# A gated Fourier mix and windowed attention on one core: when loads, subtractions and gates are listed

## The chip, the cores and the metric

The kernel runs on one core of a Trainium2 chip. The metric is device microseconds (us) of that core for one execution, as the median of several runs; lower is better. Engines are named as in the profile: PE is TensorE's matrix multiplication and PEld its load of weights, DVE is VectorE, ACT is Scalar (ScalarE), POOL is GpSimd, SP is SyncE, which issues nearly all DMAs.

## The reference

The input x has 2048 rows of 512 columns. Two results are mixed row by row with a gate g:

```python
# Fourier part: real part of a two-dimensional DFT, by matrices
a = x @ dft_hid_re.T ;  b = x @ dft_hid_im.T
y1 = dft_seq_re @ a - dft_seq_im @ b
# attention part: 32 heads of 16, causal, window of 256
q, k, v = split(x @ wqkv)
p = softmax(where(0 <= i - j < 256, q @ k.T / 4, -1e9))
y2 = (p @ v) @ wo
g = sigmoid((x * gate_w).sum(-1, keepdims=True))
out = g * y1 + (1 - g) * y2
```

All of it is float32.

## The kernel before, in words

**Split products.** A float32 matrix is split into a high part in the format fp32r (Scalar's cast, `hi_of`, line 84) and a low part, matrix minus high part (`lo_of`, line 87, on VectorE or GpSimd). A product is then three multiplications: high by high, high by low, low by high (`TERMS`, line 31).

**Two streams of work.** The attention runs over 128 steps n (8 groups of heads times 16 blocks of 128 rows). In each step `s_head` (line 312) multiplies q by k for the maxima of the rows, which VectorE reduces (line 328), and, nine steps later (`LAG`), `t_head` (line 372) multiplies again with the maxima in the matrix, Scalar takes exponentials (line 382), GpSimd masks (lines 388 and 392), and `pv` (line 396) multiplies by v. The dense part (`dense`, line 513) is a generator that yields after every matrix multiplication, and `fill` (line 733) takes a quota of its multiplications into each step of the attention. The dense part makes in turn: q, k and v (`qk_proj`, `v_proj`), b = -x times the imaginary matrix (`ab_proj` with i = 1, written to DRAM as `ab_scr1_0` to `ab_scr1_15`, 128x1024 each, high part beside low part), the other q and k, a (`ab_proj` with i = 0, of which twelve tiles stay in SBUF in `big`), then 16 row blocks of the first sequence matrix times a (`c_block`, the last two as a pair in `c_pair`), kept in DRAM as `r_scr0`, and 16 of the second times b. The sequence matrices come in pieces of 128x1024 (`raw`, `piece_load`), split by `piece_split` (line 453). Last come the rows of the output: attention times wo (`wo_run`, line 689), mixed with the gate, and stored.

**Order.** The program order is written out by the kernel itself. A clock `now` counts ticks: one for each dense multiplication, 0.7 for each quarter of a step. `defer(ticks, fn, ...)` (line 65) lists a function that many ticks later. Each engine works through its own instructions in that order. All `ld` (line 77) are on SyncE, so a DMA that must wait for a buffer or for one of the eight queues' earlier transfers holds those listed behind it.

**Places that matter here.**
- *b's tiles.* The last pair of blocks of the first matrix (`c_pair(0, 14, ..., True)`) frees the tiles of a one after the other. At chunk k, `load_next` is deferred by 5k ticks (line 506) and loads the tile of b whose number is `SC[k]`; `SC` is 4, 5, ..., 15, 0, 1, 2, 3 (line 466). TensorE's first use is in `c_pair(1, 0, ...)`, in that order.
- *Ring loads.* q and k of a group of heads are written to DRAM (`qk_scr`) by `qk_evict` (line 231) from a tile `hl`, of which there are three. `ring_load` (line 265) reads them, laid out by head, into `ring0` and `ring1`, in eight DMAs, for 512 rows of one group, ahead of their use. `m_rows` (line 332) writes the rows' maxima to `m_scr` in four DMAs and reads them back into the ring 20 ticks later.
- *Splits of pieces.* `split_raw` (line 94) lists two casts and two subtractions on halves of 512 columns at distances given by `at_` and `step`; with `pool` 1 GpSimd takes the first subtraction and VectorE the second, with 2 GpSimd takes both. The first pieces have `pool` 1: `piece_split(1, 1, 2)` and `piece_split(2, 9, 3)` (lines 582 and 583).
- *Gates.* `gate` (line 178) multiplies 512 columns of a row block of x by gate_w with a running sum, on VectorE, two in every second `sb` at ticks 3 and 7 (lines 567 to 569); `gate_exp` and `gate_end` make g from the sums.
- *wo.* `wo_load` (line 638) loads a quarter of wo and lists its split 20 and 23 ticks later.
- *Start.* Three warm-up multiplications on a tile of zeros (line 127), then `qk_first` (line 240): the first q and k, in 24 multiplications over four pieces of x of 128 columns (`XT[dk, 0]`, tiles `big`) and four pieces of the weights (`wq0`, tiles `hi` and `lo`), all split. Scalar makes the high parts, VectorE x's low parts, GpSimd the weights' low parts. GpSimd then fills a part of `ring1` with ones (line 157).
- *End.* `wo_run` for row block 15: twelve multiplications of 512 columns, one instruction of VectorE (line 706), one store.

Of the kernel before, what the change touches and what calls it, by code (L numbers as in the profile page):

```python
# [35 lines left out]
def fnet_window_mix(ctx: ExitStack, tc: tile.TileContext, xT, x, wqk, wv, wr, wi, cr, ci, wo, gw, out):  # L36
# [83 lines left out]
    def pt_tile(shape, dt=F32):  # L120
        return at.tile(shape, dt, name="pt", tag="pt", bufs=NPT)
# [17 lines left out]

    wraw = pt_tile([P, 1024])  # L140
    wq0 = [st.tile([P, 1024], F32R, name=h) for h in ("hi", "lo")]
    for dk in range(DK):
        c = slice(dk * 256, dk * 256 + 256)
        nc.scalar.dma_start(wraw[:, c], wqk[0][:, c])
    load_x_first(0)
    for dk in range(DK):
        c = slice(dk * 256, dk * 256 + 256)
        t = XT[dk, 0] = big.tile([P, 2, 512], F32R, name="big")
        raw = XRAW.pop((dk, 0))
        hi_of(wq0[0][:, c], wraw[:, c])  # L150
        hi_of(t[:, 0], raw)
        lo_of(wq0[1][:, c], wraw[:, c], wq0[0][:, c], True)
        lo_of(t[:, 1], raw, t[:, 0])

    ring = [const.tile([P, 2, S], F32R, name=f"ring{i}") for i in range(2)]
    for h in range(2):
        nc.gpsimd.memset(f(ring[1][64 * h + 32:64 * h + 64]), 1.0)

# [7 lines left out]

    gl = const.tile([P, 16], F32, name="gl")
    g1 = const.tile([P, 16], F32, name="g1")
# [8 lines left out]

    def gate(tb):
        t = GX[tb // 2][:, HALVES[tb % 2]]
        nc.vector.scalar_tensor_tensor(t, t, 1.0, gwb, op0=OP.mult, op1=OP.mult,  # L180
                                       accum_out=gl[:, tb:tb + 1])
        if tb == 15:
            defer(8, gate_exp)

    def gate_exp():
        e = const.tile([P, 16], F32, name="ge")
        nc.scalar.activation(e, gl, AF.Exp, scale=-1.0)
        defer(8, gate_end, e)
# [5 lines left out]

    rows = [False]

    def acc():
        return [ps_d.tile([P, 512], F32, name=f"d{h}", tag=f"d{h}", bufs=2) for h in range(1 + rows[0])]

# [40 lines left out]
    def qk_first(w):  # L240
        accs = [acc() for _ in range(2)]
        n = 0
        for t, dk in zip((0, 0, 1, 0, 2, 1, 0, 2, 1, 2, 1, 2), (0, 1, 0, 2, 0, 1, 3, 1, 2, 2, 3, 3)):
            a, b = ((0, 0), (1, 0), (0, 1))[t]
            for i in range(2):
                c = dk * 256 + i * 128
                mm(accs[i], w[a][:, c:c + 128], XT[dk, 0][:, b], n == 0, n == 11)
            n += 1
        return accs
# [15 lines left out]
    def ring_load(g, ss):  # L265
        sl = slice(ss * 512, (ss + 1) * 512)
        for h in range(2):
# [245 lines left out]
    def dense():  # L513
        wraw = [load_raw(wv[i]) for i in range(2)]
# [3 lines left out]
        wvs = [split_raw(r) for r in wraw]  # L518
        for i in range(2):
# [17 lines left out]
        for g in range(1, NG):  # L537
# [23 lines left out]
            if g == 1:  # L561
                for sb in range(16):
# [75 lines left out]
    def wo_load(g):  # L638
# [50 lines left out]
    def wo_run():  # L689
# [9 lines left out]
        r = wo_r.pop(tb)  # L699
        ps = ps_a.tile([P, 512], F32, name="t", tag="st")  # L700
        n = 0
        for g in range(NG):
            for a, b in TERMS:
                mm([ps], OHL[sb][g][:, a, c * P:(c + 1) * P], WO[g][b], n == 0, n == 11)
                n += 1
        nc.vector.scalar_tensor_tensor(r, ps, g0[:, tb:tb + 1], r, op0=OP.mult, op1=OP.add)
        defer(3, ld, out[tb], r)
        if c == 3:
# [121 lines left out]
```

## Time and profile before

| | |
|---|---|
| median of 3 runs | 816.08 us (815.92 to 816.9) |
| the profiled execution | 818.41 us, of which the span of recorded work is 816.7 us |
| PE busy | 799.0 us, 98% of the span |
| PEld / DVE / ACT / POOL busy | 691.9 / 484.7 / 436.6 / 421.9 us |
| moved by DMA | 164.06 MB, 201 GB/s over the span |
| mean granted clock of TensorE | 0.998 of full speed |

In the profile a row such as `549.73 9.40 SPq L78 DMA_DIRECT2D ring<-qk_scr x8` is the start and the duration in us, the engine or its queue (`SPq` is SyncE issuing), the line, the operation, output and inputs by the program's names, and how many instructions are joined in the row. Brackets such as `[3.11 <-DMA big<-ab_scr]` hold the time for which the engine had been idle, and what it was waiting for. In the view of waits the columns are: who waits for whom, us in total, how many times, the longest.

### The profile page before, as it was taken

The page shows a single profiled execution, that of the slowest core. Times are in us where ns is not written, and L with a number is a line of the kernel's source. Part 1 is how long each engine was busy: PE and PEld are TensorE (multiplying, and loading weights), DVE is VectorE, ACT ScalarE, POOL GpSimd, SP SyncE. Part 2 cuts the span into 40 slices and gives each one's busy share as a digit, 9 for nine tenths or more (in the row PEclk, how much of TensorE's full clock was granted, in tenths as well). Part 3 has the DMA queues.
Part 4 walks back from the last instruction along what each step waited for, and adds up shares of the span by engine and source line. Part 5 has one row for each costly group of instructions (what it writes and reads, how often), then busy time and mean ns, then how long its engine had stood idle before and what let it go on. Part 6 is the DMA issues. An engine that isn't in the chain of part 4 may idle for free.

```text
span 816.7 us, 22895 instructions
## 1 busy us (share of the span) xinstructions
PE 799.0 (98%) x8706; PEld 691.9 (85%) x8706; DVE 484.7 (59%) x1427; ACT 436.6 (53%) x892; POOL 421.9 (52%) x692
## 2 busy tenths in 40 slices
PE   9999999999999999999999999996999999999998
PEld 6789988889888988889888888984899988888886
DVE  4288878887776675546655655453655572245552
ACT  6334766667766665656666556553555555523110
POOL 6002666566666665666566666553666567600000
PEclk9999999999999999999999999999999999999999
DMA  7766687786885256657755554889665646478882
GB/s 277 252 173 205 199 280 245 258 266 215 250 255 179 61 165 176 187 163 194 222 148 143 163 152 129 266 268 297 180 175 141 177 127 195 161 239 259 269 239 84
DMA packets 92046, 164.06 MB, mean 201 GB/s; under 512 B 35296, under 2 KB 35936, under 8 KB 91808
## 3 DMA queue, kind: packets, MB, share of 16 engines
q1 hardware_dynamic: 90496, 160.50, 64.6%
q10 hardware_dynamic: 1440, 2.10, 0.7%
q8 instruction: 69, 1.13, 0.6%
q14 instruction: 41, 0.34, 0.2%
HBM read 109.84 MB, written 57.16 MB: 204 GB/s over the span
## 4 chain that ended last, share of the span: by engine, by line
PE 88%; DMA 6%; SPq 2%; DVE 1%; issue 1%; ACT 0%; POOL 0%; ACTq 0%; DVEq 0%; POOLq 0%
PE d L206 56%; PE d L202 9%; PE o L407 8%; PE t L202 5%; PE t L381 5%; PE s L325 4%; SPq L78 2%; DMA ring<-qk_scr 2%; DMA big<-ab_scr 2%; DMA qk_scr<-hl 1%; DMA raw<-x 1%; PE t L127 1%; DMA es<-wo 1%; DVE sm L328 1%; DMA ring<-m_scr 0%
## 5 line engine op out<-in xcount | busy, mean ns | idle before, releaser
L206 PE MATMUL d<-big,hi 64*128 64x512 f32 x2240 | 392.2, 395 | 6.7 <-DMA big<-ab_scr 6.6
L328 DVE CUSTOM_DVE_ANT_0 sm<-s,mask 128x384 f32<-128x384 f32 (+2 forms) x512 | 270.6, 529 | 143.8 <-PE s L325 83.9
L382 ACT ACTIVATE pt<-t 128x384 f32<-128x384 f32 (+2 forms) x512 | 237.7, 471 | 167.6 <-PE t L381 89.2
L206 PEld LDWEIGHTS d<-big,hi 64*128 64x128 f32 x2240 | 233.5, 186 | 32.4 <-DMA big<-ab_scr 9.6
L206 PE MATMUL d<-big,lo 64*128 64x512 f32 x1120 | 240.6, 393 | 0.0
L388 POOL TENSOR_SCALAR_AFFINE_SELECT pt<-pt 128x256 f32<-128x256 f32 x256 | 109.5, 428 | 180.8 <-ACT pt L382 164.2
L87 POOL TENSOR_TENSOR lo<-raw,hi 128x512 fp32r<-128x512 f32 x118 | 153.0, 1307 | 25.6 <-ACT hi L84 25.2
L381 PE MATMUL t<-ring,ring 50*128 50x384 f32 (+2 forms) x512 | 162.9, 329 | 3.2 <-ACT pt L382 1.4
L325 PE MATMUL s<-ring,ring 48*128 48x384 f32 (+2 forms) x512 | 163.1, 327 | 2.1 <-DVE nm L328 2.1
L206 PEld LDWEIGHTS d<-big,lo 64*128 64x128 f32 x1120 | 124.0, 186 | 11.5 <-issue 0.2
L206 PE MATMUL d<-hi,big 64*128 64x512 f32 x656 | 119.7, 392 | 0.0
L325 PEld LDWEIGHTS s<-ring,ring 48*128 48x128 f32 x512 | 92.3, 184 | 12.1 <-DVE nm L328 4.6
L381 PEld LDWEIGHTS t<-ring,ring 50*128 50x128 f32 x512 | 91.2, 184 | 11.7 <-ACT pt L382 2.2
L84 ACT CAST hi<-raw 128x512 fp32r<-128x512 f32 x146 | 87.4, 616 | 9.2 <-issue 7.9
L392 POOL TENSOR_SCALAR_AFFINE_SELECT pt<-pt 128x256 f32<-128x256 f32 x224 | 91.6, 409 | 0.0
L87 POOL TENSOR_TENSOR hl<-es,hl 128x512 fp32r<-128x512 f32 x34 | 44.8, 1319 | 72.7 <-ACT hl L84 68.9
L206 PEld LDWEIGHTS d<-hi,big 64*128 64x128 f32 x656 | 76.1, 186 | 5.8 <-issue 0.2
L206 PE MATMUL d<-lo,big 64*128 64x512 f32 x328 | 76.2, 394 | 0.0
L407 PEld LDWEIGHTS o<-pt,vpad 64*32 64x32 f32 x2816 | 60.1, 106 | 18.6 <-issue 4.6
L407 PE MATMUL o<-pt,vpad 64*32 64x320 f32 (+5 forms) x2816 | 74.0, 348 | 0.0
L414 DVE TENSOR_TENSOR os<-o,os 128x512 f32<-128x512 f32 x32 | 22.1, 691 | 70.3 <-ACT os L413 68.7
L211 ACT ACTIVATE es<-d 128x512 f32<-128x512 f32 x69 | 41.2, 597 | 25.0 <-PE d L206 22.7
(64 smaller groups left out, 705.4 us busy)
## 6 DMA issues: line engine op xcount, KB each, us to landing
qk_scr<-hl SPq DMA_DIRECT2D x32, 512.0 KB
ring<-qk_scr SPq DMA_DIRECT2D x128, 128.0 KB
raw<-cr SPq DMA_DIRECT2D x32, 512.0 KB
raw<-ci SPq DMA_DIRECT2D x32, 512.0 KB
ab_scr<-hl SPq DMA_DIRECT2D x20, 512.0 KB
big<-ab_scr SPq DMA_DIRECT2D x20, 512.0 KB
ring<-qk_scr SPq DMA_DIRECT2D x128, 64.0 KB
u_scr<-os SPq DMA_DIRECT2D x32, 256.0 KB
```

The lines of the kernel that those rows point to most:

```text
L84: nc.scalar.copy(hi, raw)
L87: (nc.gpsimd if pool else nc.vector).tensor_sub(lo, raw, f(hi))
L202: nc.tensor.matmul(pss[0], w, x, start=start, stop=stop)
L206: nc.tensor.matmul(pss[h], w[r], x[r], start=start, stop=stop)
L211: nc.scalar.activation(t, pss[0], AF.Copy, scale=scale)
L325: nc.tensor.matmul(ps[:, :w], ring[0][r, p, jb * P:(jb + 1) * P], ring[1][r, p, k0:k0 + w], start=True, stop=True)
L328: nc.vector.tensor_tensor_reduce(out=sm[:, :w], in0=ps[:, :w], in1=mask[:, WIN - w:], scale=1.0, scalar=3e38, op0=OP.add, op1=OP.min, accu ...
L381: nc.tensor.matmul(ps[:, :w], ring[1][r, p, q0:q0 + P], ring[0][r, p, q0:q0 + w], start=True, stop=True)
L382: nc.scalar.activation(pt[:, j, :w], ps[:, :w], AF.Exp, scale=-1.0)
L388: nc.gpsimd.affine_select(a, a, pattern=[[0, 2], [1, P]], compare_op=OP.is_ge, fill=0.0, base=0, channel_multiplier=-1)
L392: nc.gpsimd.affine_select(a, a, pattern=[[0, 2], [-1, P]], compare_op=OP.is_gt, fill=0.0, base=0, channel_multiplier=1)
L407: nc.tensor.matmul(ot[h][32 * j:32 * j + 32, a - sb * 512:e - sb * 512], v2[r, j], pt[r, j, a - kb * P:e - kb * P], start=kb == kbs[0], st ...
```

## The change

It has seven edits; none changes what is computed, apart from rounding in the first piece.

1. b's tile of chunk k is deferred by 4k ticks, not 5k.
2. `ring_load` lists its first four DMAs as before and, except for the first group, the other four 9.5 ticks later.
3. In `split_raw`, VectorE's subtractions of a deferred split are two quarters of 256 columns, two ticks apart. Pieces 1 and 2 are split at other distances: (1, 5) and (20, 5) for `at_` and `step`, where (1, 2) and (9, 3) stood.
4. A gate's row block is done in two halves of 256 columns, each with a sum of its own, at ticks 1, 4, 7 and 10 for two row blocks; one addition joins the sums at the end.
5. wo's split is listed 32 and 35 ticks after its load.
6. At the start, piece 0 of x and of the weights is multiplied unsplit (in float32, from the tiles `pt` that the loads fill), ahead of the rest; its split, still needed later, comes last. For pieces 1 to 3, VectorE casts x's high part and subtracts the weights' low parts, and GpSimd subtracts x's low parts. The filling of `ring1` with ones is taken apart: one half now stands ahead of these on GpSimd, one behind. The accumulators of a single product now take turns between two sets of PSUM buffers (`acc`).
7. The last row block of the output is done in two halves of 256 columns: twelve multiplications, one instruction of VectorE and one store each.

The diff, cut to its core:

```diff
-                if step:
+                if step and fn is lo_of and not args[3]:
+                    for q in range(2):
+                        k = slice(256 * q, 256 * q + 256)
+                        defer(at_ + step * (n + 2) + 2 * q, fn, *(t[:, k] for t in args[:3]))
+                elif step:
...
+    ones(0)
...
+    for dk in range(1, DK):
         c = slice(dk * 256, dk * 256 + 256)
...
+        hi_of(wq0[0][:, c], wqraw[:, c])
+        nc.vector.tensor_copy(t[:, 0], x_raw[dk])
+        lo_of(wq0[1][:, c], wqraw[:, c], wq0[0][:, c])
+        lo_of(t[:, 1], x_raw[dk], t[:, 0], True)
+        if dk == 1:
+            hi_of(XT[0, 0][:, 0], x_raw[0])
+            hi_of(wq0[0][:, :256], wqraw[:, :256])
+    lo_of(XT[0, 0][:, 1], x_raw[0], XT[0, 0][:, 0])
+    lo_of(wq0[1][:, :256], wqraw[:, :256], wq0[0][:, :256], True)
+    ones(1)
...
+    def gate(tb, q):
+        t = GX[tb // 2][:, tb % 2 * 512 + q * 256:tb % 2 * 512 + q * 256 + 256]
+        nc.vector.scalar_tensor_tensor(t, t, 1.0, gwb[:, q * 256:q * 256 + 256], op0=OP.mult, op1=OP.mult,
+                                       accum_out=gl[:, q, tb:tb + 1])
...
+    def gate_sum():
+        nc.vector.tensor_add(gl[:, 0], gl[:, 0], gl[:, 1])
...
+        for i in range(2):
+            mm(accs[i], wqraw[:, i * 128:i * 128 + 128], x_raw[0], True, False)
+        for a, b, dk in ((0, 0, 1), (1, 0, 1), (0, 1, 1), (0, 0, 2), (1, 0, 2), (0, 0, 3), (0, 1, 2), (1, 0, 3), (0, 1, 3)):
...
+        half(0)
+        if g:
+            defer(9.5, half, 1)
+        else:
+            half(1)
...
-                        defer(5 * k, load_next, SC[k])
+                        defer(4 * k, load_next, SC[k])
...
-                        defer(3, gate, sb - 1)
-                        defer(7, gate, sb)
+                        for q in range(4):
+                            defer(1 + 3 * q, gate, sb - 1 + q // 2, q % 2)
...
-        piece_split(1, 1, 2)
-        piece_split(2, 9, 3)
+        piece_split(1, 1, 5)
+        piece_split(2, 20, 5)
...
-        defer(20, hi_of, d[0], raw)
-        defer(23, lo_of, d[1], raw, d[0])
+        defer(32, hi_of, d[0], raw)
+        defer(35, lo_of, d[1], raw, d[0])
...
+        w = 256 if tb == 15 else 512
+        for q in range(0, 512, w):
+            k = slice(q, q + w)
...
+                    mm([ps[:, :w]], OHL[sb][g][:, a, c * P:(c + 1) * P], WO[g][b][:, k], n == 0, n == 11)
```

SyncE's order before, where the last four tiles of b are loaded (`ab_scr1_15` is the twelfth tile in order of use, `ab_scr1_0` the thirteenth; `ev` from `r_scr0` is a row block of the first result):

```order
L78 DMA big_9995<-ab_scr1_15_133 128x1024
L78 DMA ring0_263<-qk_scr0_3_3_93 32x2x512
L78 DMA ring0_263<-qk_scr0_3_3_93 16x2x512
L78 DMA ring1_264<-qk_scr1_3_3_109 32x2x512
L78 DMA ring1_264<-qk_scr1_3_3_109 16x2x512
L78 DMA ring0_263<-qk_scr0_3_3_93 32x2x512
L78 DMA ring0_263<-qk_scr0_3_3_93 16x2x512
L78 DMA ring1_264<-qk_scr1_3_3_109 32x2x512
L78 DMA ring1_264<-qk_scr1_3_3_109 16x2x512
L78 DMA ev_10016<-r_scr0_0_190 128x512
L78 DMA big_10045<-ab_scr1_0_118 128x1024
L78 DMA m_scr26_160<-mt_10039 32x32 x4
```

The same place now:

```order
L78 DMA big_9982<-ab_scr1_15_133 128x1024
L78 DMA big_10011<-ab_scr1_0_118 128x1024
L78 DMA ring0_243<-qk_scr0_3_3_93 32x2x512
L78 DMA ring0_243<-qk_scr0_3_3_93 16x2x512
L78 DMA ring1_244<-qk_scr1_3_3_109 32x2x512
L78 DMA ring1_244<-qk_scr1_3_3_109 16x2x512
L78 DMA ev_10037<-r_scr0_0_190 128x512
L78 DMA big_10045<-ab_scr1_1_119 128x1024
L78 DMA m_scr26_160<-mt_10062 32x32 x4
L78 DMA ring0_243<-qk_scr0_3_3_93 32x2x512
L78 DMA ring0_243<-qk_scr0_3_3_93 16x2x512
```

Tile 0 of b has moved ahead of all eight ring loads, tile 1 ahead of the second four, and the writes of maxima too; tiles 2 and 3 follow behind the second four.

SyncE's order before, 20 us earlier (tile 10 of b, behind ring loads and maxima of the step before):

```order
L78 DMA ring0_263<-qk_scr0_3_2_92 32x2x512
L78 DMA ring0_263<-qk_scr0_3_2_92 16x2x512
L78 DMA ring1_264<-qk_scr1_3_2_108 32x2x512
L78 DMA ring1_264<-qk_scr1_3_2_108 16x2x512
L78 DMA m_scr25_159<-mt_9662 32x32 x4
L78 DMA big_9738<-ab_scr1_10_128 128x1024
```

And now:

```order
L78 DMA big_9683<-ab_scr1_10_128 128x1024
L78 DMA m_scr25_159<-mt_9681 32x32 x4
L78 DMA ring0_243<-qk_scr0_3_2_92 32x2x512
L78 DMA ring0_243<-qk_scr0_3_2_92 16x2x512
L78 DMA ring1_244<-qk_scr1_3_2_108 32x2x512
L78 DMA ring1_244<-qk_scr1_3_2_108 16x2x512
```

Tile 10 stands between the two parts of the ring load, ahead of the maxima.

GpSimd's order at the start before (`lo` from `pt` are the weights' low parts):

```order
L124 MEMSET mask_224 128x384
L87 ISA
L87 TENSOR_TENSOR lo_232<-pt_230,hi_231 128x256 x4
L157 MEMSET ring1_264 32x4096 x2
L159 AFFINE_SELECT mask_224<-mask_224 128x384
```

And now (`big` from `pt` are x's low parts of pieces 1 to 3):

```order
L128 MEMSET mask_224 128x384
L153 MEMSET ring1_244 32x4096
L87 ISA
L87 TENSOR_TENSOR big_247<-pt_237,big_247 128x512
L87 TENSOR_TENSOR big_248<-pt_240,big_248 128x512
L87 TENSOR_TENSOR big_249<-pt_240,big_249 128x512
L87 TENSOR_TENSOR lo_232<-pt_230,hi_231 128x256
L153 MEMSET ring1_244 32x4096
```

One memset of the ring has moved ahead of the subtractions, which now have 512 columns in three instructions where there were 256 in four.

More of the change, by code (lines that the diff above doesn't have):

```diff
@@ L143, in fnet_window_mix, with ones @@
         c = slice(dk * 256, dk * 256 + 256)
-        nc.scalar.dma_start(wraw[:, c], wqk[0][:, c])
+        nc.scalar.dma_start(wqraw[:, c], wqk[0][:, c])
     load_x_first(0)
+    ring = [const.tile([P, 2, S], F32R, name=f"ring{i}") for i in range(2)]
+    def ones(h):
+        nc.gpsimd.memset(f(ring[1][64 * h + 32:64 * h + 64]), 1.0)
+    ones(0)
+    x_raw = [XRAW.pop((dk, 0)) for dk in range(DK)]
     for dk in range(DK):
+        XT[dk, 0] = big.tile([P, 2, 512], F32R, name="big")
+    for dk in range(1, DK):
         c = slice(dk * 256, dk * 256 + 256)
[L148 to L157, printed above, removed]
+        t = XT[dk, 0]
+        hi_of(wq0[0][:, c], wqraw[:, c])
[8 more added lines that the diff above has]
+    ones(1)
     nc.gpsimd.affine_select(mask, mask, pattern=[[1, WIN]], compare_op=OP.is_gt, fill=BIG,
@@ L195, in fnet_window_mix @@
     rows = [False]
+    turn = 0
     def acc():
-        return [ps_d.tile([P, 512], F32, name=f"d{h}", tag=f"d{h}", bufs=2) for h in range(1 + rows[0])]
+        nonlocal turn
+        if rows[0]:
+            return [ps_d.tile([P, 512], F32, name=f"d{h}", tag=f"d{h}", bufs=2) for h in range(2)]
+        turn ^= 1
+        return [ps_d.tile([P, 512], F32, name="d0", tag=f"d{turn ^ 1}", bufs=2)]
     def mm(pss, w, x, start, stop):
@@ L265, in ring_load, with half @@
     def ring_load(g, ss):
-        sl = slice(ss * 512, (ss + 1) * 512)
-        for h in range(2):
+        def half(h):
+            sl = slice(ss * 512, (ss + 1) * 512)
             for i in range(2):
@@ L513, in dense @@
     def dense():
-        wraw = [load_raw(wv[i]) for i in range(2)]
+        raws = [load_raw(wv[i]) for i in range(2)]
         load_x_first(1)
```

38 lines of the change are left out of this document (15 added, 23 removed).

## The prediction, made before the changed kernel was run

> **What bounds the kernel now.** I read the page's first part, then the waits of TensorE, then the stretches where they lie.
>
> ```profile
> span 816.7 us, 22895 instructions
> ...
> PE 799.0 (98%) x8706; PEld 691.9 (85%) x8706; DVE 484.7 (59%) x1427; ACT 436.6 (53%) x892; POOL 421.9 (52%) x692
> ```
>
> TensorE is busy 98% of the span and no other engine over 60%. An edit pays only where it ends a TensorE wait, shortens TensorE's own work, or shortens the ends. The profiled execution took 818.41 us (span 816.7, 1.7 around it); the median of the plain runs is 816.08, 2.33 below. I make the sum against the profiled execution and take that offset over. About 0.2% (1.6 us) is what a measurement of this kernel can tell from no change.
>
> The view of waits, TensorE only (total us, times, longest):
>
> ```profile
> PE d L206 <- DMA big<-ab_scr: 6.6, 3, 3.1
> PE s L325 <- DVE nm L328: 2.1, 3, 1.0
> PE t L381 <- ACT pt L382: 1.4, 2, 0.8
> ...
> PE t L381 <- DVE nm L328: 0.4, 1, 0.4
> ```
>
> The largest is three waits for tiles of b that come back from DRAM. In TensorE's timeline:
>
> ```profile
> 558.86 0.73 PE L206 MATMUL d<-big,hi 64*128 64x512 f32 x4 [0.91 <-DMA big<-ab_scr]
> ...
> 563.97 1.22 PE L206 MATMUL d<-big,hi 64*128 64x512 f32 x4 [3.11 <-DMA big<-ab_scr]
> ...
> 571.58 0.73 PE L206 MATMUL d<-big,hi 64*128 64x512 f32 x4 [2.54 <-DMA big<-ab_scr]
> ```
>
> They follow each other within 13 us. The table of stretches (window, length, busy us of the engines, granted TensorE clock, DMA share, GB/s) and SyncE's timeline say why:
>
> ```profile
> 534.00:540.00 6.00, 6.00 (x90) 5.12 (x79) 3.43 (x10) 4.34 (x9) 2.17 (x5) 1.00 0.51 94
> ...
> 546.00:555.00 9.00, 8.85 (x135) 6.62 (x136) 4.21 (x17) 3.26 (x8) 4.60 (x8) 1.00 1.03 415
> 555.00:561.00 6.00, 4.95 (x72) 3.62 (x56) 2.40 (x8) 2.13 (x5) 1.56 (x5) 1.00 0.89 165
> ...
> 564.00:567.00 3.00, 3.00 (x14) 2.21 (x16) 0.57 (x2) 0.49 (x1) 0.43 (x2) 0.50 0.78 261
> ```
>
> ```profile
> 529.07 6.54 SPq L78 DMA_DIRECT2D ring<-qk_scr  x8
> ...
> 548.96 0.37 SPq L78 DMA_DIRECT2D big<-ab_scr  x1
> 549.73 9.40 SPq L78 DMA_DIRECT2D ring<-qk_scr  x8
> ...
> 560.35 0.43 SPq L78 DMA_DIRECT2D big<-ab_scr  x1
> 560.89 1.76 SPq L78 DMA_DIRECT2D m_scr<-mt  x4
> ```
>
> SyncE lists in order. Eight ring loads held it from 549.73 to 559.13, and the last four tiles of b (0 to 3) stood behind them. The ring loads are slow: 165 GB/s in 555 to 561 against 415 in 546 to 555, where b's tiles and the pieces moved. Before that, in 534 to 540, the DMA engines were half idle (share 0.51). After the wait of 3.11 the granted clock is 0.50 for one stretch.
>
> **The change part by part.**
>
> *b's loads at 4k ticks, ring loads in two parts.* In the new order b's tile 10 goes out ahead of the four writes of maxima, into the idle stretch, and tile 0 (first to stand behind the eight ring loads) directly behind tile 15. What is at stake: 0.91 + 3.11 + 2.54 = 6.56 us, and the half clock: from 563.97 on some 3 us at 0.50, at most 1.5 lost, I take 1.4. Together 8.0. Next, what is late then. A tile of b is 0.52 MB, 1.3 us at 415 GB/s; half a ring load is 0.39 MB, 2.4 us at 165. Tile 15 was there at 558.86; with one tile already moved in the idle stretch and no ring load pressing behind I take 556.5. Tile 0 then comes at 557.8; TensorE wants it at 563.97 - 3.11 - 0.91 = 559.95, so no wait. Then half a ring (560.2), a row of r (0.26 MB, 560.8) and tile 1 at 562.1. A tile lasts TensorE six steps of 0.227 (rows of the tail, below) and some score products, 1.7 us, so tile 1 is wanted at 561.7: 0.4 late. The other half ring (564.5) and tile 2 at 565.8: wanted at 571.58 - 2.54 - 0.91 - 3.11 - 1.4 + 0.4 = 564.0, so 1.8 late. Tile 3, 1.3 later, is wanted 1.7 later: covered. Left: 2.2. **Gain 5.8**; bounds 1.5 (the tiles stay late by most of it) and 8.0 (none waits).
>
> The half ring that goes later: a tick is about 0.25 us (between the ring loads at 529.07 and 549.73 the order has four rounds of 4 x (0.7 + 3.9) ticks and 9 more, 82.6 ticks in 20.66 us). So it moves by 2.4 us and four issues, and it is used about 15 us after its listing: free as long as that stands. What queues behind it on SyncE (rows of u, x's rows, writes of q and k) stands at the same place as before. The maxima go four issues earlier; nothing waits for them here.
>
> *Subtractions in halves, later splits, gates in column halves.* VectorE's and GpSimd's rows where TensorE waited for VectorE:
>
> ```profile
> 147.06 1.70 DVE L180 SCALAR_TENSOR_TENSOR raw<-raw,ev 128x512 f32<-128x512 f32 x1
> ...
> 298.32 1.79 DVE L87 TENSOR_TENSOR lo<-raw,hi 128x512 fp32r<-128x512 f32 x1
> ```
>
> ```profile
> 146.91 1.29 POOL L87 TENSOR_TENSOR hl<-es,hl 128x512 fp32r<-128x512 f32 x1
> ...
> 298.27 1.30 POOL L87 TENSOR_TENSOR big<-es,big 128x512 fp32r<-128x512 f32 x1 [1.85 <-ACT big L84]
> ```
>
> The gate that began at 147.06 lasted until 148.76, GpSimd's subtraction until 148.20: 1.14 us of the 1.70 is waiting for GpSimd, 0.56 its own. At 298.32 it is 1.25 and 0.54. Scores' reductions queue behind, and TensorE waits for these:
>
> ```profile
> 165.86 0.44 PE L325 MATMUL s<-ring,ring 48*128 48x384 f32 x1 [0.82 <-DVE nm L328]
> ...
> 300.64 0.44 PE L325 MATMUL s<-ring,ring 48*128 48x384 f32 x1 [0.96 <-DVE nm L328]
> ```
>
> Of the 2.1 in three waits 0.96 and the remaining 0.31 stand behind pieces 1 and 2, 1.3 together; 0.82 and the 0.4 in t's scores stand behind gates, 1.2 together. Half as many columns takes some 0.3 off each block, and a reduction can stand between two halves. The splits of pieces 1 and 2, four subtractions within 17 ticks before, now spread over 37, two quarters of 0.5 us apart. Of the pieces' 1.3 I take **1.0** (bounds 0.3 and 1.3), of the gates' 1.2 **0.5** (0 and 1.2; the rows of x still land when they land). Some 30 extra instructions lie in VectorE's idle 41%; without it they would cost about 0.1 each.
>
> The Trainium skill, in "SBUF — State Buffer", section "Who interferes with whom", says that a VectorE instruction with two SBUF inputs and a GpSimd instruction that reads SBUF exclude each other for a whole instruction, and that a VectorE copy or cast may too. By that each half would still wait for a whole subtraction: I would take 0.6 and 0.4 for pieces and gates and -0.1 for the start below, 0.8 less in the sum (808.3). The rows above agree with the first half of the rule; for the cast no row of this trace shows it.
>
> *wo's splits 12 ticks later.* Scalar waits on wo's load, and t's exponentials behind it:
>
> ```profile
> 365.38 0.62 ACT L84 CAST hl<-es 128x512 fp32r<-128x512 f32 x1 [2.46 <-DMA es<-wo]
> 249.28 0.62 ACT L84 CAST hl<-es 128x512 fp32r<-128x512 f32 x1 [2.13 <-DMA qk_scr<-hl]
> ```
>
> 12 ticks are 3.0 us, more than the 2.46: one of TensorE's two waits (1.4 together, the longest 0.8) goes. **Gain 0.75** (0.4 at the least). The second row stays; its bounds are -1.2 (the late ring half lands ahead of that write) and +0.7, I take 0.
>
> *First piece unsplit.* Rows of the start, TensorE's, then Scalar's first cast of x's second piece and GpSimd's memset of the ring's ones:
>
> ```profile
> 1.27 4.21 PE L127 MATMUL t<-mask 128*128 128x384 f32 x6 [1.27 <-POOL mask L124]
> 5.25 2.34 PE L202 MATMUL d<-big,hi 128*128 128x512 f32 x4
> 7.42 0.64 PE L202 MATMUL d<-big,lo 128*128 128x512 f32 x2
> ...
> 12.69 0.50 PE L202 MATMUL d<-hi,big 128*128 128x512 f32 x1 [0.46 <-ACT pt L211]
> ```
>
> ```profile
> 5.74 0.61 ACT L84 CAST big<-pt 128x512 fp32r<-128x512 f32 x1
> ```
>
> ```profile
> 9.31 7.09 POOL L157 MEMSET ring<- 32x4096 f32 x2
> ```
>
> Three unsplit products of 384 columns are six passes, from 1.27 to 5.25: 0.66 each, 0.88 over 512 columns. Two products of two passes make 3.54 at this pace. The pace doubles at about 7.4 (four split products 2.34 before, two 0.64 after). From 5.25 on 2.15 us run slow, the other 1.39 in 0.70: done at 8.1, where six split products stood. Eighteen steps of 0.227 (row of the tail, below) end at 12.2, and V's first product no longer waits for a PSUM buffer: 0.5 gained on 12.69. But x's low parts are now on GpSimd:
>
> ```profile
> L87 POOL TENSOR_TENSOR lo<-raw,hi 128x512 fp32r<-128x512 f32 x118 | 153.0, 1307 | 25.6 <-ACT hi L84 25.2
> ```
>
> x's second piece is there at 5.74, its high part some 0.5 later; one memset of 3.5 that now stands ahead on GpSimd ends at 4.7. Three of 1.31 from 6.2 on end at 10.1 alone, and at about 12 if VectorE's six instructions between must take turns; the last group of products starts at 11.7. **Gain 0.2**, bounds -0.6 and +0.6.
>
> *Last row in halves.*
>
> ```profile
> 809.86 2.20 PE L202 MATMUL t<-hl,pt 128*128 128x512 f32 x9
> 811.90 0.84 PE L202 MATMUL t<-es,pt 128*128 128x512 f32 x3
> ```
>
> ```profile
> 40.07 0.28 PE L325 MATMUL s<-ring,ring 48*128 48x256 f32 x2
> 40.19 0.40 PE L206 MATMUL d<-lo,big 64*128 64x512 f32 x2
> ```
>
> ```profile
> L328 DVE CUSTOM_DVE_ANT_0 sm<-s,mask 128x256 f32<-128x256 f32 x32 | 13.3, 415 | 8.0 <-PE s L325 5.3 <-PE t L381 2.2
> 812.78 0.75 DVE L706 SCALAR_TENSOR_TENSOR ev<-t,g,ev 128x512 f32<-128x512 f32 x1 [1.97 <-PE t L202]
> 813.56 0.33 SPq L78 DMA_DIRECT2D out<-ev  x1
> ```
>
> Nine products take 2.04, 0.227 each, twelve 2.72. A step of 256 columns takes 0.12 (40.07 to 40.19), 24 make 2.88: 0.16 lost. VectorE's last instruction falls from 0.75 to about the 0.42 that a reduction of 256 columns takes: 0.33. The store, 3.1 us from its issue to the span's end, moves half the bytes: 0 to 0.4, I take 0.1. **Gain 0.3**, bounds 0 and 0.6.
>
> Sum: 5.8 + 1.0 + 0.5 + 0.75 + 0.2 + 0.3 = 8.55. Profiled 818.41 - 8.55 = 809.9; less the offset, **807.5**.
>
> **The rivals.** *Listing is not the limit:* the DMA engines are full (1.03) in 546 to 555, so b's last tiles come almost as late. For: the share; against: the idle 534 to 540. Then 6.5 of the 8.0 stay and the rest comes: 816.08 - 4.3 = 811.8. *Everything goes:* no b tile waits, the start gains 0.6, nothing else collides: 8.0 + 1.3 + 1.2 + 0.75 + 0.6 + 0.6 = 12.4, 803.7. Against: the arithmetic of tile 2. *Slower:* the late ring half, 2.4 us of slow packets, lands ahead of a write whose buffer Scalar waits for, as at 249.28; eight ring loads between 90 and 260 us have such writes behind them. From four on (8.55 / 2.4 = 3.6) it eats the gain; at five it gives 816.08 + 12.0 - 8.55 = 819.5. Against: only one such wait in 816 us, and the bytes ahead of those writes are the same as before. *No effect:* b's waits move unchanged and small ones arise for those that go, 815.5.
>
> **How the numbers follow.** Forecast 0.56, listing 0.20, everything 0.12, no effect 0.05, slower 0.07. Faster 0.88, same 0.05, slower 0.07. The range reaches from beyond "everything" (803.0; the bounds allow a little more) to beyond "listing" (814.0), and leaves out the last two and the tails.
>
> **What would show it.** Right: tile 0 listed before 551, no b wait over 2 us in 545 to 570 and granted clock 1.00 there; no wait at 299 and 365; V's first product at 12.1 to 12.8; twelve halves in 1.4. Wrong: waits for ring or hl tiles that were not there, b's waits still summing to over 4 us, or a last half with steps of 0.2.

## The result, and the profile after

| | before | after |
|---|---|---|
| median | 816.9 us (814.75 to 821.81, 17 runs) | 822.05 us (818.61 to 827.18, 17 runs) |
| ratio to before | | 1.0062, 95% interval 1.0043 to 1.0082 |
| profiled execution, span | 818.41, 816.7 | 822.24, 820.5 |

The change makes the kernel slower by 0.6%, some 5 us. 807.5 was forecast, in a range from 803.0 to 814.0. One execution each of g2 (972.52 us) and h1 (1116.47) below, and one of the kernel before (874.0), ran at a granted clock of 0.66 to 0.85 and are left out of the times and ratios (with its own, g2's median is the 808.17 that an expectation below names). The page of the changed kernel, first part, then TensorE's waits (who for whom: us in total, times, longest):

```profile
span 820.5 us, 22966 instructions
...
PE 800.2 (98%) x8716; PEld 699.7 (85%) x8716; DVE 496.0 (60%) x1488; ACT 435.1 (53%) x889; POOL 425.1 (52%) x692
```

```profile
PE d L229 <- DMA big<-ab_scr: 6.9, 3, 3.5
PE s L352 <- DVE nm L355: 2.6, 4, 1.2
PE t L408 <- DVE nm L355: 2.5, 4, 0.9
...
PE d L225 <- DVE lo L87: 1.1, 2, 0.7
```

The waits for b, 6.6 us before, are 6.9. The waits for VectorE's reductions (`nm`) have doubled, 2.5 to 5.1 over both kinds of scores. The waits for Scalar (1.4) are gone. TensorE's waits for b's tiles, and the stretches around them (window, length, busy us of PE, PEld, DVE, ACT, POOL, granted clock, DMA share, GB/s):

```profile
564.20 0.73 PE L229 MATMUL d<-big,hi 64*128 64x512 f32 x4 [1.28 <-DMA big<-ab_scr]
...
569.50 0.51 PE L229 MATMUL d<-big,hi 64*128 64x512 f32 x2 [3.46 <-DMA big<-ab_scr]
...
574.12 1.22 PE L229 MATMUL d<-big,hi 64*128 64x512 f32 x4 [2.16 <-DMA big<-ab_scr]
```

```profile
561.00:566.00 5.00, 3.72 (x32) 2.61 (x28) 2.02 (x8) 1.73 (x4) 0.80 (x3) 1.00 1.06 165
566.00:572.00 6.00, 2.50 (x18) 1.57 (x16) 1.00 (x3) 1.75 (x4) 0.73 (x2) 0.91 0.64 166
572.00:580.00 8.00, 5.88 (x38) 4.88 (x40) 2.57 (x8) 1.64 (x4) 4.40 (x7) 0.64 0.84 313
```

The same three waits stand there, and the half clock lasts longer: a mean clock of 0.91 over 6 us and 0.64 over 8 us is 2 x (0.09 x 6 + 0.36 x 8) = 6.8 us at 0.50, against some 3.4 before. SyncE's issues around it:

```profile
535.88 5.33 SPq L78 DMA_DIRECT2D m_scr<-mt  x4
541.27 2.31 SPq L78 DMA_DIRECT2D ring<-qk_scr  x4
...
544.10 0.43 SPq L78 DMA_DIRECT2D big<-ab_scr  x1
...
559.47 0.33 SPq L78 DMA_DIRECT2D big<-ab_scr  x1
560.80 5.15 SPq L78 DMA_DIRECT2D m_scr<-mt  x4
566.20 3.57 SPq L78 DMA_DIRECT2D ring<-qk_scr  x4
569.82 0.90 SPq L78 DMA_DIRECT2D big<-ab_scr  x2
```

The four writes of maxima, 3.15 and 1.76 us before, take 5.33 and 5.15: tiles of b and the first four ring loads are still under way, and SyncE waits for the earlier transfers of the same queues (for tiles of b 3.1 us of the first and 4.0 of the second). Behind that come the second four ring loads, and behind these b's tiles 2 and 3, at 569.82. Tile 1, issued at 559.47, ended TensorE's wait at 569.50: ten microseconds, in a stretch that moved 165 GB/s.

The gates, in the stretch from 128 to 178 us; in this order: two of TensorE's six waits for VectorE, one half gate on VectorE, GpSimd's subtraction beside it, and all gates as a group of after and of before (us in total, mean ns):

```profile
151.61 0.32 PE L408 MATMUL t<-ring,ring 50*128 50x128 f32 x1 [0.78 <-DVE nm L355]
...
167.49 0.44 PE L352 MATMUL s<-ring,ring 48*128 48x384 f32 x1 [1.24 <-DVE nm L355]
```

```profile
131.50 1.51 DVE L194 SCALAR_TENSOR_TENSOR raw<-raw,ev 128x256 f32<-128x256 f32 x1
```

```profile
131.15 1.58 POOL L87 TENSOR_TENSOR hl<-es,hl 128x512 fp32r<-128x512 f32 x1 [1.20 <-ACT hl L84]
```

```profile
L194 DVE SCALAR_TENSOR_TENSOR raw<-raw,ev 128x256 f32<-128x256 f32 x32 | 19.8, 633 | 4.3 <-DMA raw<-x 4.3
```

```profile
L180 DVE SCALAR_TENSOR_TENSOR raw<-raw,ev 128x512 f32<-128x512 f32 x16 | 13.8, 860 | 0.7 <-DMA raw<-x 0.7
```

A half of 256 columns that began at 131.50 ended 0.28 us after GpSimd's subtraction did. Thirty-two halves take 19.8 us where sixteen whole gates took 13.8.

To see where the time goes, I take the starts of VectorE's reductions of scores in each trace: from the 81st to the 121st (52.7 us before; the gates lie there) and from the 413th to the 449th (54.0 us before; b's loads lie there). This table of differences from the kernel before is used below. Each number is of one execution. Kernels that leave the gates and the ring loads there as they were lie between -1.1 and +0.3 in the gate stretch; kernels that leave b's loads and the ring loads lie between -1.4 and +0.4 in b's; and b's loads at 4k with whole ring loads among them give -1.4 to -4.6. So 1 us in the first column, or 2 in the second, says nothing by itself.

| kernel | gate stretch, us | b stretch, us |
|---|---|---|
| after | +4.18 | +1.96 |
| e1 b's loads at 4k | +0.28 | -3.60 |
| e2 ring in two parts | +0.89 | +2.35 |
| e3 gates in halves | +1.95 | -0.21 |
| e4 start | +0.01 | -0.51 |
| f1 after, ring whole | +1.48 | -3.86 |
| f3 b at 4k, ring in parts but not at b | +1.97 | -4.57 |
| f2 after, ring and gates whole | +0.02 | -1.40 |
| g1 b at 4k, ring in parts 4 ticks apart | -0.02 | +1.31 |
| g2 best | -1.04 | -4.10 |
| g4 quarters and later splits | -0.99 | -0.42 |
| h2 b at 4k, the later ring load among b's tiles in parts | -1.08 | -0.10 |
| i1 as f3, 4 ticks apart | -0.01 | -3.39 |
| i2 gates in halves, low parts of b's tiles on VectorE | +1.26 | -1.43 |

### The profile page after: what moved, and what is told of

It reads as the page before. It is cut to its first block, busy times and chain, and to the rows that moved or that the text cites. A ratio compares the mean times of both kernels' runs of the same rounds, so it can differ in the third digit from the quotient of the medians.

```text
span 820.5 us, 22966 instructions
## 1 busy us (share of the span) xinstructions
PE 800.2 (98%) x8716; PEld 699.7 (85%) x8716; DVE 496.0 (60%) x1488; ACT 435.1 (53%) x889; POOL 425.1 (52%) x692
## 4 chain that ended last, share of the span: by engine, by line
PE 86%; DMA 6%; DVE 4%; issue 2%; SPq 1%; ACT 0%; POOL 0%; ACTq 0%; DVEq 0%; POOLq 0%
PE d L229 55%; PE d L225 8%; PE o L434 8%; PE t L225 5%; PE t L408 5%; PE s L352 5%; DMA big<-ab_scr 2%; DVE sm L355 1%; DVE raw L194 1%; DMA ring<-qk_scr 1%; DMA raw<-x 1%; SPq L78 1%; DMA raw<-ci 1%; DVE lo L87 1%; DMA pt<-wqk 1%
## 5 line engine op out<-in xcount | busy, mean ns | idle before, releaser
L229 PEld LDWEIGHTS d<-big,hi 64*128 64x128 f32 x2240 | 240.4, 186 | 28.5 <-DMA big<-ab_scr 8.3
L229 PE MATMUL d<-big,lo 64*128 64x512 f32 x1120 | 244.8, 393 | 0.0
L229 PEld LDWEIGHTS d<-big,lo 64*128 64x128 f32 x1120 | 129.0, 186 | 10.1 <-issue 0.2
```

The source lines that it names most:

```text
L229: nc.tensor.matmul(pss[h], w[r], x[r], start=start, stop=stop)
```

## The experiments

The ratios are to the kernel before on the same chip, with 95% intervals; 0.1% is 0.8 us. Differences in us are taken from the ratios.

**One edit alone.** *e1:*

```diff
-                        defer(5 * k, load_next, SC[k])
+                        defer(4 * k, load_next, SC[k])
```

> The kernel before, with b's loads deferred by 4k ticks and nothing else. Theory 'the second half of the ring load, now behind the maxima, is what keeps b's tiles late' expects that this edit alone does what was forecast of it: TensorE's waits for b's tiles fall from 6.6 us to under 3 and the time by 3 to 6 us. Theory 'the transfers themselves are the limit there, whatever the order' expects the waits at 6 to 8 us and the time within 1 us of before.

812.27 us, ratio 0.9944 (0.9923 to 0.9964), 4.6 us faster. TensorE's waits for b:

```profile
PE d L206 <- DMA big<-ab_scr: 3.6, 2, 2.5
```

3.6 us, a little over the 3 that was set. The edit alone does most of what was forecast of it, so the order does count.

*e2:*

```diff
+        half(0)
+        if g:
+            defer(9.5, half, 1)
```

> The kernel before, with the ring load in two parts and nothing else. Theory 'late half': SyncE stands at the writes of maxima until the first four ring loads are through (some 5 us, as at 535.88 to 541.27 in the changed kernel), and what is listed behind comes later: 3 to 6 us slower, b's waits 7 us or more, and waits for VectorE between 128 and 260 us that the kernel before does not have. Theory 'order of no weight': within 1 us of before.

822.09 us, ratio 1.0061 (1.0039 to 1.0083), 5.0 us slower, as the theory of the late half has it. Two of its signs were off: b's waits were 5.8 in the profiled execution, not 7, and between 128 and 260 us TensorE waited for VectorE only where it does in the kernel before, one wait having grown from 0.82 to 1.72. The granted clock over the 40 us from 540 was 0.87, some 10 us at half, against 0.96 before. This execution took 818.93, the shortest of the twelve, so that its trace cannot show the whole of the 5.0 us. SyncE's waits for VectorE's transposed maxima (`mt`), here and in the kernel before:

```profile
SPq L78 <- DVE mt L343: 27.7, 18, 5.1
```

```profile
SPq L78 <- DVE mt L338: 6.6, 4, 5.1
```

Eighteen waits of SyncE where there were four, 21 us more. Seventeen of them have four ring loads listed behind the writes; the last, of 5.1 us, is in both kernels and has none.

*e3:*

```diff
-                        defer(3, gate, sb - 1)
-                        defer(7, gate, sb)
+                        for q in range(4):
+                            defer(1 + 3 * q, gate, sb - 1 + q // 2, q % 2)
```

> The kernel before, with the gates in column halves at ticks 1, 4, 7, 10 and nothing else. Theory 'a half waits as long for GpSimd as a whole': TensorE's waits for VectorE between 128 and 185 us rise from 1.2 us to 2.5 or more, and the time by 1 to 3 us. Theory 'only the loads behind the late ring half make the gates late': waits at most 1.2 us, time within 0.7 us of before.

818.54 us, ratio 1.0029 (1.0005 to 1.0053), 2.4 us slower, with the kernel before's ring loads. So the gates cost by themselves. TensorE's waits for VectorE in the gate stretch rose from 1.2 to 2.3 us, a little under the 2.5 that was set.

*e4 (the unsplit first piece, its engines, the memset and the accumulators in turn; the diff is that of the change):*

> The kernel before, with the first piece unsplit, x's low parts on GpSimd and the accumulators in turn, and nothing else. By the profile of the changed kernel (0.73 us of waiting for VectorE's low parts of v's weights where 0.46 stood, and V's second product 0.24 us earlier or later) the time stays within 0.7 us of before; the rival that the exchange of PSUM buffers or of engines costs something later expects 1 us or more.

814.8 us, ratio 0.9973 (0.9951 to 0.9994), 2.2 us faster, more than the 0.7 expected. The first reduction of scores starts 0.18 us earlier in its trace, and neither stretch of the table has gained. The two traces differ by 4.7 us, and 2.8 of these are waits that the one of before has at 105 (1.34), 249 (0.68) and 365 (0.75); g4, which leaves the start alone, lacks all three as well. Whether the start is worth 0.2 or 2 us stays open.

**Undoing.** *f1, the changed kernel with `half(1)` directly behind `half(0)`:*

> The changed kernel with the ring load in one part again, all else as changed. Theory 'the late half undoes the gain of b's loads and delays x's rows': the 5 us of the ring edit and what it takes from the 4.6 us of the earlier b loads come back; 812 to 816 us, and between the 412th and the 448th reduction of scores 3 to 4 us less than in the kernel before, where the changed kernel has 2 more. Rival 'the edits do not interact': 822.05 less 5.0 is 817.

813.34 us, ratio 0.9969 (0.9952 to 0.9985). The ring edit alone makes the difference between 0.6% slower and 0.3% faster, 0.0093 or 7.6 us: more than alone (5.0), though by no more than the intervals allow. By the table the larger part lies in b's stretch (+1.96 against -3.86), where the ring edit takes away the gain of b's loads, the smaller in the gates' (+4.18 against +1.48).

*f2, the gates whole as well:*

> The changed kernel with the ring load in one part and the gates whole at ticks 3 and 7, all else as changed. Both edits that cost time alone (5.0 and 2.4 us) are out: 808 to 812 us, faster than either kernel. If something else in the change also costs (pieces 1 and 2 split later, wo later, the unsplit first piece), it comes out above 812.3, the time of the earlier b loads alone.

811.78 us, ratio 0.9942 (0.9919 to 0.9964). Faster than either kernel, but no faster than e1, which has only one of its edits: something in the rest costs, or what should have helped does not.

**Why the ring's second part costs.** *f3, e1 and e2 together, with the two ring loads among b's tiles whole:*

```diff
+        if g and (g, ss) not in ((6, 2), (6, 3)):
+            defer(9.5, half, 1)
```

> The kernel before with b's loads at 4k ticks and the ring load in two parts, except for the two ring loads that stand among b's loads, which stay whole there. Theory 'the price of the ring edit lies at b's tiles': 811 to 814 us, like the earlier b loads alone (812.3). Theory 'half of the price lies in the 32 other places, before all between 100 and 260 us where x's rows and the maxima share the queue': 814 to 817 us.

815.96 us, ratio 0.9996 (0.9976 to 1.0015): 4.2 us above e1, though b's stretch keeps its gain. (26 ring loads are in two parts here, not the 32 of the text above.) A large part of the price lies elsewhere; TensorE's two waits in the gate stretch, 0.39 and 0.82 in the kernel before, have grown with gates that are whole:

```profile
147.26 0.32 PE L386 MATMUL t<-ring,ring 50*128 50x128 f32 x1 [1.50 <-DVE nm L333]
...
164.70 0.44 PE L330 MATMUL s<-ring,ring 48*128 48x384 f32 x1 [1.72 <-DVE nm L333]
```

*g1, the second part 4 ticks behind the first everywhere (`defer(4, half, 1)`), which puts it ahead of the maxima:*

> The kernel before with b's loads at 4k ticks and the ring load in two parts everywhere, but the second part 4 ticks later, so that it stands ahead of the writes of maxima as before and not behind them. Theory 'it is the place behind the maxima that costs (SyncE waits there for VectorE, 2.8 us at 154.56 in the ring edit alone, with the second part behind it, and the queues run idle)': 811 to 814 us, as with the earlier b loads alone (812.3). Theory 'two parts cost by themselves, wherever the second stands': 815 us or more, as with the parts 9.5 ticks apart outside b's place (816.0).

816.21 us, ratio 0.9996 (0.9974 to 1.0017): by the time, my theory fell. The table says that only half of it did: the gate stretch is as before (-0.02), and the loss is all in b's stretch. So I tried the two apart.

*i1, f3 with `defer(4, half, 1)`:*

> The kernel before with b's loads at 4k ticks and the ring load in two parts 4 ticks apart, so that the second stands ahead of the maxima, except for the two ring loads among b's tiles, which stay whole. It differs from f3 (816.0) only in 4 ticks for 9.5. Theory 'away from b the price is the place behind the maxima': 811 to 813.5 us, as with the earlier b loads alone, and no waits of 1.5 us for VectorE near 145 and 162. Theory 'two parts cost by themselves': 815 to 817.

812.13 us, ratio 0.9956 (0.9938 to 0.9975), as e1, and the two waits are 0.37 and 0.83. The interval of f3 begins where this one ends. Away from b two parts cost nothing if the second stands ahead of the maxima, and 0.0040 or 3.3 us if it stands behind them. SyncE's issues in the same place, f3 first, then i1:

```profile
149.89 1.87 SPq L78 DMA_DIRECT2D ring<-qk_scr  x4
...
154.97 1.71 SPq L78 DMA_DIRECT2D m_scr<-mt  x4
156.73 1.83 SPq L78 DMA_DIRECT2D ring<-qk_scr  x4
...
164.32 1.24 SPq L78 DMA_DIRECT2D raw<-x  x2
```

```profile
150.00 2.01 SPq L78 DMA_DIRECT2D ring<-qk_scr  x4
...
152.52 3.23 SPq L78 DMA_DIRECT2D ring<-qk_scr  x4
155.84 1.76 SPq L78 DMA_DIRECT2D m_scr<-mt  x4
...
162.19 1.31 SPq L78 DMA_DIRECT2D raw<-x  x2
```

In f3 SyncE issues nothing from 152.2 to 154.97, since the maxima are not there; the ring's second part follows only then, and x's second pair of rows, which the gate needs, goes out 2 us later. In i1 the same part goes out while the maxima are being made.

*h1 and h2, e1 with only one ring load in two parts, 9.5 ticks apart: the earlier of the two among b's tiles, (6, 2), then the later, (6, 3):*

> The kernel before with b's loads at 4k ticks; of all ring loads only the earlier of the two among b's tiles (tile 10 between its parts) is taken in two parts, 9.5 ticks apart. If the price at b's place comes from here (SyncE held at the maxima, tiles 11 to 15 issued 3 us later), 816 to 819 us; if it comes from the later one, 811 to 814.

> The same with only the later of the two (tile 1 and the maxima between its parts) in two parts. If the price at b's place comes from here (tile 1 moves together with slow ring packets, and tiles 2 and 3 wait for both), 816 to 819 us; if from the earlier one, 811 to 814. If each gives half, both lie at 814 to 816.

813.92 us, ratio 0.9967 (0.9941 to 0.9994), and 813.34 us, ratio 0.9962 (0.9939 to 0.9986): 1.9 and 1.5 us above e1, below the 814 to 816 that was set for half each. e1's 0.9944 lies in both intervals, so neither load is shown to cost alone; that the two together do is measured by g1 against i1, 3.3 us, with intervals that just touch. What happens there is seen in g1 and, without the edit, in e1, SyncE's issues again:

```profile
552.74 0.34 SPq L78 DMA_DIRECT2D big<-ab_scr  x1
554.16 5.19 SPq L78 DMA_DIRECT2D ring<-qk_scr  x4
559.48 3.98 SPq L78 DMA_DIRECT2D m_scr<-mt  x4
563.50 1.98 SPq L78 DMA_DIRECT2D big<-ab_scr  x2
```

```profile
548.44 9.93 SPq L78 DMA_DIRECT2D ring<-qk_scr  x8
...
558.93 0.43 SPq L78 DMA_DIRECT2D big<-ab_scr  x1
559.46 1.76 SPq L78 DMA_DIRECT2D m_scr<-mt  x4
561.27 0.90 SPq L78 DMA_DIRECT2D big<-ab_scr  x2
```

Tile 1 goes out at 552.74, 6.2 us earlier than in e1 (558.93), and the multiplication that waits for it still starts at 563.18, in e1 at 562.75. It runs beside the ring's second part. The maxima wait for both, and tiles 2 and 3 go out at 563.5, in e1 at 561.3. In h2, with the maxima between the two parts, tile 1 went out at 552.34 and was waited for until 560.86. That the sharing with ring loads is the cause is argued from these times.

**Whether b's last waits can go.** *g3, the best version (below) with b's loads at 3k, which puts tiles 1 and 2 ahead of the ring load; h3 and h4, the best version with that ring load listed 12 or 20 ticks later, so that one or none of b's tiles stands behind it:*

```diff
-            ring_load(g, ss)
+            if (g, ss) == (6, 3):
+                defer(12, ring_load, g, ss)
+            else:
+                ring_load(g, ss)
```

> The same with b's loads at 3k ticks, which puts tiles 1 and 2 of b ahead of the ring loads too. Theory 'what stands behind the ring loads and the maxima comes late': the remaining waits for b's tiles (3 to 4.5 us with 4k) fall below 2 us and at most one unit of half clock is left; 2 to 4 us faster than with 4k. Rival 'the transfers are the limit now': no faster than with 4k.

> The best version so far (b's loads at 4k, ring load whole, gates whole, halves of 512; 808.17) with the later of the two ring loads listed 12 ticks later as a whole, so that tiles 1 and 2 of b, a row block and the maxima stand ahead of it and tile 3 behind it. Theory 'the tile behind the ring's slow packets waits some 3 us, whichever it is': no gain, 807 to 810 us, a wait of 2 to 3.5 us for tile 3 in place of tile 1.

> The same 20 ticks later, so that all of b's tiles stand ahead of that ring load. Same theory: the wait is gone (under 1 us for b's tiles in all), no unit of half clock, 3 to 5 us faster: 803.5 to 805.5. Rival 'the tiles cannot come faster whatever stands behind them': still 2 us or more of waiting, 807 to 809.

810.25 us, ratio 0.9932 (0.9907 to 0.9956); 810.43 us, ratio 0.9920 (0.9896 to 0.9943); 809.05 us, ratio 0.9927 (0.9899 to 0.9955). None gains on the best version's 0.9902. In g3 and h3 TensorE waits 3.1 and 3.7 us for tile 3, which stands behind the ring load there, as it waits 3.4 in the best version for tile 1. In h4 no tile waits, but:

```profile
PE t L395 <- DMA ring<-m_scr: 2.4, 1, 2.4
PE s L339 <- DMA ring<-m_scr: 1.5, 1, 1.5
```

The maxima's way back stands behind the ring load now and waits 3.9 us. So of my two theories neither held as put: tiles can come faster (no wait for them is left), and it earns nothing where 3 to 5 us were set. The wait has passed to what is listed next, and the half clock lasts 6.8 us in this trace (none was expected; 3.4 in the best version's).

**Gates and quarters.** *f4, halves directly after one another at ticks 3 and 7:*

```diff
+                            defer(3 + 4 * (q // 2), gate, sb - 1 + q // 2, q % 2)
```

> The kernel before with the gates in column halves, the two halves of a row block directly after one another at ticks 3 and 7, where the whole ones stand. Theory 'listing the first half at tick 1 is what costs (it meets rows of x that have not landed, 1.97 and 2.29 us of waiting in the changed kernel)': within 1 us of before. Theory 'each half can be caught by GpSimd for a whole subtraction, so four pieces meet it more often than two': 1.5 us or more above before.

817.5 us, ratio 1.0028 (1.0010 to 1.0047), 2.3 us: the early tick is not what costs, halving is.

*i2, e3 with the subtractions of b's tiles on VectorE in place of GpSimd:*

> The kernel before with the gates in column halves at ticks 1, 4, 7, 10, and the low parts of b's tiles subtracted on VectorE where GpSimd did it, so that GpSimd has no subtraction beside the gates. Theory 'a half that starts beside GpSimd's subtraction waits for the whole of it': no gate half lasts over 0.7 us (1.51 and 1.50 in the changed kernel), and TensorE's waits for VectorE between 128 and 185 us fall under 1 us, though VectorE has 16 more instructions of about 0.8 us; 814 to 817 us. Rival 'the gates are long for another reason': halves of 1.5 us stay and the time rises by the added work, 819 or more.

818.12 us, ratio 1.0030 (1.0011 to 1.0049). The time is no better than e3's; VectorE has sixteen more instructions to do, and I had set 814 to 817. TensorE's waits for VectorE in the gate stretch are 1.6 us, 2.3 in e3, where I had set under 1. The mechanism that it was made for shows clearly, in the group of the gates:

```profile
L180 DVE SCALAR_TENSOR_TENSOR raw<-raw,ev 128x256 f32<-128x256 f32 x32 | 14.3, 455 | 0.0
```

14.3 us where e3 has 20.5, and no half over 0.63 us where e3 has seven over 1. It is GpSimd's subtraction that makes the long halves long. That the long halves are what costs the 2.4 us is not shown by it: without them the time is e3's. The sixteen added instructions may cost what was gained; no run separates the two.

*g4, the quarters and the later splits of pieces 1 and 2 alone; g2, the changed kernel with the ring load and the gates whole and the subtractions in halves of 512 columns, but the later splits kept (`piece_split(1, 1, 5)`, `piece_split(2, 20, 5)`):*

> The kernel before with the subtractions in quarters and pieces 1 and 2 split later, nothing else. The forecast had 1.0 us of gain. Theory 'quarters are caught as often as they save': the waits for VectorE at 299 to 302 fall from 1.3 us to under 0.6, new ones near 92, 111 and 228 add 1 to 1.6; time within 1 us of before.

> The changed kernel with the ring load in one part, the gates whole, and the subtractions in halves of 512 columns again (the other distances of pieces 1 and 2 stay). Theory 'two quarters can each be caught by GpSimd (0.93 us of waiting for VectorE at 228.77 in the changed kernel, which the kernel before does not have)': about 1 us faster than with the quarters (811.78), so 810 to 811.5, and no wait for VectorE near 224. Rival 'quarters are worth what was forecast': 812.3 or more.

g4: 816.41 us, ratio 1.0007 (0.9985 to 1.0029). The waits at 299 to 302 fall from 1.3 to 0.4, and new ones come at 92 (0.46, for GpSimd), 98 (0.19), 112 (0.21) and 223 (0.92). g2: **807.15 us, ratio 0.9902 (0.9871 to 0.9933)**, the fastest of all and below the 810 to 811.5 that was set; f2, which differs only by the quarters, has 0.9942, with intervals that overlap. All of TensorE's waits in it, but for one of 0.4 for VectorE:

```profile
PE d L221 <- DMA big<-ab_scr: 3.5, 2, 3.4
PE t L127 <- POOL mask L124: 1.3, 1, 1.3
PE d L217 <- DVE lo L87: 0.7, 1, 0.7
```

Neither the waits at 299 to 302 nor those of g4 are there, where f2's trace has 2.0 us of them (0.46 at 92, 0.18 at 112, 0.93 at 224, 0.42 at 299). The later splits are what helps; the quarters cost, 2.0 us by these waits and 3.3 by the ratios.

## Why the prediction was wrong

Taken apart by g2, f2, f1 and the change itself, each against before: the edits that help give 0.0098 (8.0 us), the quarters take 0.0040 (3.3), the gate halves 0.0027 (2.2), the ring in two parts 0.0093 (7.6). They add up to the result, 5.1 us slower, because each is counted from the one before it. Each is known to 2 or 3 us only: the ring's share is far above that, the quarters' and the gate halves' are not.

- **The step that failed** is "free as long as that stands" of the ring's late half, together with "The maxima go four issues earlier; nothing waits for them here". I asked who waits for the maxima, and not what the maxima wait for. Their write waits on VectorE, SyncE stands still with it, and the half ring now stood behind it (18 waits for 4; f3 against i1, 3.3 us). Among b's tiles it waits instead for earlier transfers of the queues (the writes took 5.33 and 5.15 us, and tiles 2 and 3 went out at 569.82). A term put at nothing cost 7.6 us (f1). The rival "slower" had the late half as its mechanism, but placed it ahead of writes whose buffer Scalar waits for; that wait did not grow (the longest 0.44 us, 2.13 before), and 0.07 was too little for a slow transfer moved past a write that itself waits. Two of the signs of being wrong came: b's waits of 6.9 us, over 4, and tile 0 listed after 553.5, not before 551.
- **b's loads.** "Gain 5.8" was measured as 4.6 without the ring edit (e1), and the waits left are 3.6 where I left 2.2. With the ring edit none of it stayed. The term's arithmetic gave each tile 1.3 us and each half ring 2.4, one after the other. They run side by side at 165 GB/s: tile 1 took 10 us, and in e1, sent behind the whole ring load, 3.8 (558.93 to 562.75). The kernel before showed it already: tile 15, issued at 548.96, was waited for until 558.86. Nor did the ring loads hold SyncE for 9.4 us of their own, as the prediction read it: of the time from 549 to 560 SyncE waited 4.4 us for tiles of b and 2.1 for pieces that were still in flight, 0.3 for ring loads. The Trainium skill, in "SBUF — State Buffer", section "Door 1: The DMA port swizzle", says that a transfer of few partitions reaches only some of the ports; the ring loads have 16 and 32 partitions, and the 165 GB/s agree, against 415 in 546 to 555 of the kernel before. That a wide transfer beside them slows down too is what these traces add.
- **Gates**, 0.5 forecast, cost 2.4. The step "half as many columns takes some 0.3 off each block" looked at the gate's own time. A half beside GpSimd's subtraction lasts as long as that does, and thirty-two instructions meet it more often than sixteen (seven over 1 us against three). That this makes up the 2.4 us is argued, and i2 does not bear it out by the time; that halving costs is measured (e3, f4). By the rule that the prediction cited from the Trainium skill ("SBUF — State Buffer", section "Who interferes with whom": exclusion for a whole instruction), a half can wait as long as a whole gate, and the half of 1.51 us above agrees. I priced it as 0.1 us less and not as a loss. Exclusion was seen for the cast too, which the trace of before did not show: at the start VectorE's cast of x took 1.52 us beside a subtraction and 0.43 without:

```profile
5.32 0.43 DVE L163 CAST big<-pt 128x512 fp32r<-128x512 f32 x1 [5.32 <-DMA pt<-xT]
...
8.04 1.52 DVE L163 CAST big<-pt 128x512 fp32r<-128x512 f32 x1
```

```profile
7.86 1.41 POOL L87 TENSOR_TENSOR big<-pt,big 128x512 fp32r<-128x512 f32 x1 [0.70 <-DVE big L163]
```

- **Pieces**, 1.0 forecast: the distances earned it, the quarters took it back (g4, g2). They are held as the halves of gates are: in f2 two quarters run from 221.51 to 223.79, beside two subtractions of GpSimd that end at 223.51.
- **wo**, 0.75: not shown. The changed kernel has no wait at 365 and 0.9 us less between the 241st and the 301st reduction. But e4, f4, g1, g4 and h2, which leave wo alone, have no such wait either and 0.7 to 1.0 us less, while e2 and f3 have the wait (0.89 and 1.23). No run has this edit alone.
- **Start**, 0.2: the trace agrees (0.12 at the first reduction, with a new wait of 0.73 for VectorE's low parts), in its bounds; e4's 2.2 is open.
- **Tail**, 0.3: from the start of the last row to the end 6.84 us before (809.86 to 816.7) and 6.35 after (814.15 to 820.5), 0.5, in its bounds. The last instruction of VectorE:

```profile
817.22 0.48 DVE L736 SCALAR_TENSOR_TENSOR ev<-t,g,ev 128x256 f32<-128x256 f32 x1 [0.95 <-PE t L225]
```

## What to carry to other kernels

When an issue in an in-order queue moves past another, ask what that other one waits for, not only who waits for it: a slow transfer that used to run while the queue waited for an engine now starts after the wait. Before cutting an instruction in two to shorten a blocking wait, ask whether the wait scales with the instruction; here it was the other engine's whole instruction, and two pieces were two chances to be caught. For the pieces, moving the splits apart in time helped; for the gates no run tried it. And a change of several edits is worth taking apart: four of the seven and half of a fifth made the kernel 1.0% faster, and the rest took more than that.

## What was not expected of the hardware

The half clock behind b's waits comes in steps: 0, 3.4, 6.8 or 10.2 us at 0.50 in different executions (e3, before, after, e2), for 5.8 to 7.4 us of waiting for b in all four, so that one execution's wait says little of its price. And a transfer of 0.52 MB took 10 us beside ring loads of 16 and 32 partitions, while the DMA engines showed a share of 1.06.
